# Shared key and value blocks loaded once, queries and stores issued at another place in the step, in a fused attention and mixture-of-experts kernel

## The chip, the cores and the metric

The kernel runs on one core of one Trainium2 chip. The metric is the device time of one execution in microseconds (us); before the change it is 421.25 us, the median of three runs (419.26 to 423.34).

## The reference

Eight batches of eight heads, 576 positions, head size 64. Heads 0 to 3 attend to the last 32 positions, heads 4 to 7 to every fourth of the last 128. The result, seen as 4608 rows of 512, goes through a layer that skips some rows and sends each of the others to one of eight experts.

```python
scores = scale * np.matmul(q, k.transpose(0, 1, 3, 2))
mask_plain = (rel >= 0) & (rel < window)                                        # window = 32
mask_dil = (rel >= 0) & (rel < window * dilation) & (rel % dilation == 0)       # dilation = 4
attn = softmax(np.where(masks, scores, -1e9));  x = attn @ v                    # rows of B*S, H*D
do_compute = x @ w_skip > 0
e_idx = argmax(x[do_compute] @ w_gate);  gate_w = softmax(...)[e_idx]
out = x;  out[do_compute] += gate_w * (relu(x @ w1[e_idx]) @ w2[e_idx])
```

## The kernel before

**Attention, 24 steps.** A pair of batches (`bp`, four of them) has two halves: half 0 is the four heads with the plain window, half 1 the four dilated ones, whose positions are reordered so that their keys too lie side by side. A half is cut in three parts (`PARTS`), and a part is one step `t`: t = 0, 1, 2 is half 0 of the first pair, 3, 4, 5 its half 1, and so on. A step handles three groups of 64 queries; each block of 32 queries needs two blocks of 32 keys and of 32 values, its own and one before it. Inputs come from DRAM arranged by step (`laid_out`).

**Loads.** `load("kv", t)` (L143) issues two DMAs on SP that fill a tile `kvs[t % 3]` with the keys of step t and the values of step t - 2 (`LAG`); `load("q", t)` one DMA for the queries, into one of three buffers. Neighbouring groups use the same key or value block; before the change a block that a step needs twice at a border is stored twice in DRAM, and the blocks at the border of two parts are loaded by both steps. `share` (L158) copies the values that matmuls on the other half of the partitions need into a tile `shared`: ACT copies partitions 0 to 63 and POOL 64 to 127.

**A step.** The order is written out in `STEP` (L474): T transposes the weights of step t (`turn`: PE, copied out of PSUM by ACT); R computes the scores of t + 2 (`product`, L188); E is the exponential of t + 1 on ACT; V and v split a piece of expert weights (ACT, DVE); C is `share(t + 1)`; S masks and reduces the scores of t + 2 on DVE (L199, L202) and subtracts the maximum on POOL (L204); A sums the values (L246); X transposes the outputs of t - 1 (L302) and copies them by ACT to `xT`; D divides on DVE (L256 to L260); each w gives one piece of the router's work on the pair before. PE's last matmul of `sums(t)` is followed by L302, so L302 marks the start of the next step on PE.

**SP's order.** At the start of step t SP issues `load("kv", t + 4)`, `load("q", t + 4)`, up to eight stores of finished rows (`EACH`; a half 0 is stored whole in two DMAs, a half 1 in sixteen), and in steps 12 to 19 one piece of the first expert's weights (L900). SP issues in order. The kv load waits for `sums(t - 1)`, for the copies out of its tile, and every DMA on SP uses one of eight completion semaphores in rotation, so that it waits for the DMA issued eight before it to have landed.

**After the attention.** `finish` does the router's work on the last pair, fills its waits with the first expert's matmuls, and `Experts.run` does the other experts. `Router.prepare` makes the router's constants on POOL in three pieces, one each at the end of steps 1, 2 and 3.

Of the kernel before, what the change touches and what calls it, by code (L numbers as in the profile page):

```python
# [20 lines left out]
P = 128  # L21
# [5 lines left out]
W = 32  # L27
# [10 lines left out]
KN = 4 * max(KEYS)  # L38
NEG = -8.0e9
LAG = 2  # L40
EACH = 8
# [7 lines left out]
def window(half, g, sub):  # L49

    lower, upper = ((0, 2), (1, 2), (1, 3))[g] if half else (g, NB + g + sub)
    return slice(4 * half * sub + lower, 4 * half * sub + upper + 1, upper - lower)


def swapped(half, g, sub):
    return g % NB == 1 if half else sub == 0
# [46 lines left out]
class Attention:  # L103
# [7 lines left out]
    def __init__(self, tc, consts, qkv, out, prepare):  # L111
# [11 lines left out]
        self.shared = [self.kp.tile([P, 2, DN], F32, name=f"shared{i}") for i in range(3)]  # L123
# [19 lines left out]
    def load(self, kind, t):  # L143
# [8 lines left out]
        a = VN if kind == "k" else 0  # L152
        n = VN + 4 * KEYS[t // PARTS % 2] if "k" in kind and t < last else VN
        if t < last + LAG:
            for hh in range(2):
                self.nc.sync.dma_start(out=self.kvs[t % 3][hh::2, hh, a:n], in_=self.qkv[t][hh::2, QN + a:QN + n])

    def share(self, t):  # L158
# [4 lines left out]
        loaded, shared = self.loaded(t), self.shared[t % 3]  # L163
        n, up = (D + 1, 0) if t // PARTS % 2 else (2 * (D + 1), D + 1)
        for copy, rows, a in (nc.scalar.copy, slice(0, 64), n), (nc.gpsimd.tensor_copy, slice(64, P), up):
            copy(out=shared[rows].rearrange("c h (x d) -> c h x d", d=n),  # L166
                 in_=loaded[rows].rearrange("c h (x d) -> c h x d", d=2 * n)[:, :, :, a:a + n])

    def scores(self, half, t, g0):
# [7 lines left out]
        k = self.keys(t).rearrange("c h (r b s i) -> c h r b s i", r=2, b=2, i=W)  # L177
        ps = []

        def product():  # L180
            ps.append(self.ps.both("s"))
            for g in range(NB):
                for r in range(2):
                    n, j = divmod(2 * g + r, 4)
                    for b in range(2):
                        for sub in range(2):
# [3 lines left out]
                                rhs=k[:, :, r, b, window(half, g, sub)], start=True, stop=True,  # L190
# [21 lines left out]
    def values(self, t):  # L212

        if t // PARTS % 2:
            shared, loaded = (v.rearrange("c h (r b y x d) -> c h r b y x d", r=2, b=2, y=2, d=D + 1)
                              for v in (self.shared[t % 3], self.loaded(t)))
            return (0, 2, 1), lambda r, b, g, y: shared[:, :, r, b, y, 0] if g == 1 else loaded[:, :, r, b, y, g // 2]
        shared, loaded = (v.rearrange("c h (r b x d) -> c h r b x d", r=2, b=2, d=D + 1)
                          for v in (self.shared[t % 3], self.loaded(t)))
        return (0, 1, 2), lambda r, b, g, y: loaded[:, :, r, b, 1 + g] if y else (  # L220
            shared[:, :, r, b, g - 1] if g else loaded[:, :, r, b, 0])
# [103 lines left out]
    def run(self, router, experts, early, finish):  # L325
# [56 lines left out]
        product(1)  # L382
        for _ in range(3):
            shift(1)
# [1057 lines left out]
```

## Time and profile before

| | |
|---|---|
| time, median of three | 421.25 us |
| time of the profiled execution | 420.55 us, of which the span of its instructions is 418.5 us |
| attention, steps 0 to 23 on PE | 11.5 to 159.4 us |
| TensorE busy over the span | 380.8 us (91%) |
| VectorE, ScalarE, GpSimd busy | 64%, 51%, 33% |
| DMA | 88.92 MB, mean 212 GB/s |

A row of a timeline reads: start, duration of the whole merged row in us, engine, line, operation, output and inputs, shape, count, and in brackets how long the engine had been idle and what released it. SPq is SP's queue of DMA issues.

### The profile page before, as it was taken

What the parts mean: (1) busy time and instruction counts of PE and PEld (TensorE: products, weight loads), DVE (VectorE), ACT (ScalarE), POOL (GpSimd) and SP (SyncE); (2) the same over time, 40 slices, a digit from 0 to 9 for tenths busy, and PEclk for the clock granted to TensorE, in tenths of its full rate; (3) what the DMA queues carried; (4) which work ended last, traced back from release to release, by engine and by line L of the source; (5) the groups of instructions that cost most, each with busy time, mean ns of one, the idle gap of its engine ahead of it and who ended that gap; (6) DMA issues with size and microseconds to landing.
All of it is one profiled execution on the core that took longest, in us unless ns stands there. A gap on an engine that the chain in (4) does not pass through costs nothing.

```text
span 418.5 us, 11103 instructions
## 1 busy us (share of the span) xinstructions
PE 380.8 (91%) x4257; PEld 325.8 (78%) x4257; DVE 268.7 (64%) x552; ACT 211.9 (51%) x435; POOL 137.2 (33%) x213
## 2 busy tenths in 40 slices
PE   5888698799699858989999999999999999999993
PEld 3777567678577746877998899899889879898982
DVE  5766438968996894888544835726726837768540
ACT  6576456676568664615427125424515516456420
POOL 7884513574346431032207212112113113141001
PEclk9999889999889999999999999999999999999998
DMA  7989778978998866373756354473663664766001
GB/s 235 402 316 366 250 209 290 336 226 233 341 367 295 275 183 212 117 221 122 264 169 210 130 198 140 163 248 102 201 225 116 203 212 154 275 207 219 25 2 44
DMA packets 40101, 88.92 MB, mean 212 GB/s; under 512 B 5315, under 2 KB 14547, under 8 KB 38504
## 3 DMA queue, kind: packets, MB, share of 16 engines
q1 hardware_dynamic: 36424, 77.02, 55.4%
q0 software_dynamic: 3616, 11.11, 7.9%
q8 instruction: 35, 0.57, 0.5%
q14 instruction: 26, 0.21, 0.2%
HBM read 73.88 MB, written 14.75 MB: 212 GB/s over the span
## 4 chain that ended last, share of the span: by engine, by line
PE 52%; DVE 0%; POOL 0%; POOLq 0%; issue 0%
PE o L1099 25%; PE s L1028 23%; PE tp L1009 2%; PE tp L1051 1%; PE tp L1063 0%; DVE yo L1104 0%; POOL out_dram L997 0%; POOLq L1369 0%; DVE txl L1013 0%; PE s L855 0%
## 5 line engine op out<-in xcount | busy, mean ns | idle before, releaser
L1099 PE MATMUL o<-w,h 128*128 128x512 f32 (+2 forms) x320 | 103.8, 398 | 1.0 <-DVE h L1032 1.0
L997 POOL DMA_INDIRECT out_dram<-yo,write x21 | 22.5, 1070 | 154.5 <-DVE yo L1104 154.5
L1028 PE MATMUL s<-xh,w 128*128 128x256 f32 (+3 forms) x240 | 69.6, 307 | 0.5 <-DVE at_rows L771 0.5
L1028 PE MATMUL s<-xl,w 128*128 128x256 f32 (+3 forms) x240 | 69.4, 306 | 0.0
L1099 PEld LDWEIGHTS o<-w,h 128*128 128x128 f32 (+2 forms) x320 | 57.9, 184 | 14.1 <-DVE h L1032 1.4
L1031 ACT ACTIVATE h<-s 128x256 fp32r<-128x256 f32 (+3 forms) x60 | 25.9, 432 | 79.0 <-PE s L1028 54.1
L204 POOL TENSOR_TENSOR sm<-sm,mx 128x768 f32<-128x768 f32 (+1 forms) x25 | 36.0, 1439 | 39.8 <-DVE z L256 27.6
L1028 PEld LDWEIGHTS s<-xh,w 128*128 128x128 f32 x240 | 45.5, 190 | 1.1 <-DVE at_rows L771 0.6
L1028 PEld LDWEIGHTS s<-xl,w 128*128 128x128 f32 x240 | 45.5, 190 | 0.4
L188 PE MATMUL s<-kv,q 128*32 128x128 f32 x1152 | 38.7, 281 | 5.2 <-DVE sm L199 1.8
L991 POOL DMA_INDIRECT xg<-out_dram,read x24 | 26.0, 1081 | 50.8 <-DVE read L834 24.0
L916 DVE TENSOR_TENSOR w0l<-w0l,w 128x512 fp32r<-128x512 f32 x48 | 34.0, 709 | 12.3 <-ACT w L907 11.2
L188 PEld LDWEIGHTS s<-kv,q 128*32 128x32 f32 x1152 | 31.7, 112 | 11.4 <-issue 7.7
L246 PE MATMUL o<-kv,pT 128*32 128x130 f32 x768 | 35.4, 286 | 3.5 <-ACT pT L234 2.1
L916 DVE TENSOR_TENSOR w2l<-w2l,w 128x512 fp32r<-128x512 f32 x40 | 27.6, 690 | 14.4 <-ACT w L907 13.4
L916 DVE TENSOR_TENSOR w1l<-w1l,w 128x512 fp32r<-128x512 f32 x40 | 27.8, 694 | 13.5 <-ACT w L907 12.3
L1032 DVE SCALAR_TENSOR_TENSOR h<-s,h 128x256 fp32r<-128x256 f32 (+3 forms) x60 | 28.6, 476 | 11.8 <-ACT h L1031 11.7
L166 POOL COPY shared<-kv 64x1040 f32<-64x1040 f32 x24 | 26.6, 1108 | 25.8 <-DMA kv<-in_qkv_dram 18.7
L1104 DVE SCALAR_TENSOR_TENSOR yo<-o,gate,xg 128x512 f32<-128x512 f32 (+2 forms) x21 | 15.7, 749 | 29.1 <-PE o L1099 29.0
L246 PEld LDWEIGHTS o<-kv,pT 128*32 128x32 f32 x768 | 29.2, 114 | 5.2 <-ACT pT L234 2.8
L233 PE MATMUL tp<-ident,sm 128*128 128x128 f32 x144 | 24.2, 291 | 9.1 <-ACT xT L305 5.8
L1012 ACT CAST xh<-tp 128x256 fp32r<-128x256 f32 (+3 forms) x32 | 13.2, 417 | 37.4 <-PE tp L1009 37.2
(204 smaller groups left out, 755.3 us busy)
## 6 DMA issues: line engine op xcount, KB each, us to landing
kv<-in_qkv_dram SPq DMA_DIRECT2D x24, 516.0 KB, 6.5
w0l<-in_moe_w_dram SPq DMA_DIRECT2D x48, 256.0 KB, 4.4
w1l<-in_moe_w_dram SPq DMA_DIRECT2D x40, 256.0 KB, 3.9
w2l<-in_moe_w_dram SPq DMA_DIRECT2D x40, 256.0 KB, 4.2
kv<-in_qkv_dram SPq DMA_DIRECT2D x20, 484.0 KB, 5.4
q<-in_qkv_dram SPq DMA_DIRECT2D x24, 384.0 KB, 6.8
out_dram<-xh SPq DMA_DIRECT2D x8, 576.0 KB, 7.6
out_dram<-xh SPq DMA_DIRECT2D x24, 80.0 KB, 4.8
```

The source lines that it names most:

```text
L166: copy(out=shared[rows].rearrange("c h (x d) -> c h x d", d=n), in_=loaded[rows].rearrange("c h (x d) -> c h x d", d=2 * n)[:, :, :, a:a + n])
L188: nc.tensor.matmul(ps[0][p:p + W, n, 2 * KW * j:2 * KW * (j + 1)], lhsT=q[:, r, b, g, sub], rhs=k[:, :, r, b, window(half, g, sub)], start ...
L204: nc.gpsimd.tensor_tensor(out=part, in0=part, in1=top.unsqueeze(2).broadcast_to([P, n, KW, 2]), op=ALU.subtract)
L233: nc.tensor.transpose(out=tp[:, P * j:P * j + P], in_=sm[:, NB * n + j], identity=self.ident)
L246: nc.tensor.matmul(ps[0][p:p + W, n, 2 * (D + 1) * j:2 * (D + 1) * (j + 1)], lhsT=pT[:, m, p:p + W], rhs=v(r, b, g, sub), start=True, stop ...
L916: (engine or self.nc.vector).tensor_tensor(out=lo, in0=raw, in1=hi.bitcast(F32), op=ALU.subtract)
L991: self.nc.gpsimd.indirect_dma_start(out=xg, out_offset=None, in_=self.out[0:rows], in_offset=bass.IndirectOffsetOnAxis(ap=row, axis=0),)
L997: self.nc.gpsimd.indirect_dma_start(out=view, out_offset=bass.IndirectOffsetOnAxis(ap=row, axis=0), in_=yo, in_offset=None, bounds_check=N ...
L1028: nc.tensor.matmul(ps[0], lhsT=w(part, k, P * f, P), rhs=x[:, k], start=(i == 0), stop=(i == len(terms) - 1))
L1031: nc.scalar.activation(out=hh, in_=ps[0], func=AF.Relu)
L1032: return lambda: nc.vector.scalar_tensor_tensor(out=hl, in0=ps[0], scalar=0.0, in1=hh.bitcast(F32), op0=ALU.max, op1=ALU.subtract)
L1099: nc.tensor.matmul(ps[0][0:n], lhsT=h[:, ts], rhs=w(part, f, 0, DM), start=(i == 0), stop=(i == len(terms) - 1))
```

## The change

Every key block that a step needs is in its DRAM row once at most. The border block (half 0) or blocks (half 1) of a part that the part before has already loaded are no longer loaded: `follow` copies them on POOL from the tile of step t - 1 to that of step t, right behind the scores of t - 1, for parts 1 and 2 of each half. A kv DMA has 768 columns of keys for 896 (half 0) or 1024 (half 1), and in half 0 780 columns of values for 1040. `share` of a half 0 now copies all three value pairs: ACT 1560 columns for 1040, POOL 1040 and, in parts 1 and 2, 520 more from the tile of the step before. `shared` has two tiles for three. In half 0 `sums` uses `shared` for one of the two blocks of every group, so from its first matmuls on. `load("q", t + 5)` is issued behind the scores of t + 2, then up to six stores for eight and the piece of weights; at the start of a step SP issues only the kv load, until the last three steps. A half 0 is stored after each part, two DMAs each. The router's constants are made at the end of steps 3, 4 and 5. Masks and the arrangement in DRAM follow the new order of blocks (not shown).

```diff
-EACH = 8
+VS = (4 * NB * (D + 1), VN)
+NEW = 2 * NB
+KL = 4 * W * NEW
+EACH = 6
...
-        self.shared = [self.kp.tile([P, 2, DN], F32, name=f"shared{i}") for i in range(3)]
+        self.shared = [self.kp.tile([P, 2, VS[0]], F32, name=f"shared{i}") for i in range(2)]
...
-        a = VN if kind == "k" else 0
-        n = VN + 4 * KEYS[t // PARTS % 2] if "k" in kind and t < last else VN
+        a = VN if kind == "k" else VN - VS[(t - LAG) // PARTS % 2]
+        n = VN + KL if t < last else VN
...
+    def follow(self, t):
+
+        half = t // PARTS % 2
+        if t < B * PARTS and t % PARTS:
+            new, old = (self.kvs[i % 3][:, :, VN:].rearrange("c h (s k) -> c h s k", k=4 * W) for i in (t, t - 1))
+            self.nc.gpsimd.tensor_copy(out=new[:, :, NEW:NEW + 1 + half], in_=old[:, :, 1:NB + 2:NB] if half else
+                                       old[:, :, NB:NB + 1])
+
...
+        shared, loaded, older = (v.rearrange("c h (n x d) -> c h n x d", x=NB, d=D + 1) for v in (
+            self.shared[t % 2], *(self.loaded(i)[:, :, VN - VS[0]:] for i in (t, t - 1))))
+        nc.scalar.copy(out=shared[0:64].rearrange("c h n x d -> c h (n x d)"),
+                       in_=loaded[0:64].rearrange("c h n x d -> c h (n x d)"))
+        if t % PARTS:
+            nc.gpsimd.tensor_copy(out=shared[64:P, :, :, 0], in_=older[64:P, :, :, NB - 1])
...
-        return (0, 1, 2), lambda r, b, g, y: loaded[:, :, r, b, 1 + g] if y else (
-            shared[:, :, r, b, g - 1] if g else loaded[:, :, r, b, 0])
+                          for v in (self.shared[t % 2], self.loaded(t)[:, :, VN - VS[0]:]))
...
+        nc.vector.memset(self.shared[0][64:P], 0.0)
...
+        self.follow(1)
...
+        self.follow(2)
+        self.load("q", 4)
...
-            for kind in "kv", "q":
-                self.load(kind, t + 4)
-            due = len(stores) - EACH * (PARTS - 1 - part) if t < steps - 1 else 0
-            for _ in range(min(len(stores), max(EACH, due))):
-                stores.pop(0)()
+            self.load("kv", t + 4)
+            if t >= steps - PARTS:
+                for _ in range(min(len(stores), EACH)):
...
-            if WSTART <= t < WSTART + CHUNKS:
-                experts.load_next((2 * t - 2 * WSTART - (CHUNKS - 1) * (t >= WSTART + CHUNKS // 2),))
...
                     product(t + 2)
+                    self.follow(t + 3)
+                    self.load("q", t + 5)
+                    if t < steps - PARTS:
+                        for _ in range(min(len(stores), EACH)):
+                            stores.pop(0)()
+                    if WSTART <= t < WSTART + CHUNKS:
+                        experts.load_next((2 * t - 2 * WSTART - (CHUNKS - 1) * (t >= WSTART + CHUNKS // 2),))
...
-            if t:
+            if t >= PARTS:
...
-            if i == len(quads) - 1:
+            if half == 0 or i == len(quads) - 1:
                 stores += self.store_rows(bp, half, xh, g0, NB)
```

On SP, in step 13 (the kv loads of step 17, `kv_85`, and of step 18, `kv_83`), with what each row waits for (DMAHW0 to 7 are the eight completion semaphores); before, from the query load on:

```order
L149 DMA q<-in_qkv_dram 128x768 [waits DMAHW2_49]
L292 DMA out_dram<-xh 16x5x256 [waits DMAHW3_49]
L292 DMA out_dram<-xh 16x4x256 [waits DMAHW4_49]
L292 DMA out_dram<-xh 16x4x256 [waits DMAHW5_49]
L292 DMA out_dram<-xh 16x5x256 [waits DMAHW6_49]
L292 DMA out_dram<-xh 16x5x256 [waits DMAHW7_49]
L292 DMA out_dram<-xh 16x4x256 [waits DMAHW0_49]
L292 DMA out_dram<-xh 16x4x256 [waits DMAHW1_49]
L292 DMA out_dram<-xh 16x5x256 [waits DMAHW2_49]
L900 DMA w0l_1656<-in_moe_w_dram 128x512 [waits DMAHW3_49]
L156 DMA kv_83<-in_qkv_dram 64x1936 [waits PE_49,DMAHW4_49,Activation_49,Pool_49]
```

Between the query load and the next kv load stand eight stores and a piece of weights. The same place after the change:

```order
L159 DMA kv_85<-in_qkv_dram 64x1808 [waits PE_49,DMAHW7_49,Activation_49,Pool_49]
L159 DMA kv_85<-in_qkv_dram 64x1808 [waits DMAHW0_49]
L152 DMA q<-in_qkv_dram 128x768 [waits DMAHW1_49,PE_49]
L310 DMA out_dram<-xh 16x4x256 [waits DMAHW2_49]
L310 DMA out_dram<-xh 16x5x256 [waits DMAHW3_49]
L310 DMA out_dram<-xh 16x5x256 [waits DMAHW4_49]
L310 DMA out_dram<-xh 16x4x256 [waits DMAHW5_49]
L310 DMA out_dram<-xh 16x4x256 [waits DMAHW6_49]
L310 DMA out_dram<-xh 16x5x256 [waits DMAHW7_49]
L926 DMA w0l_1735<-in_moe_w_dram 128x512 [waits DMAHW0_49]
L159 DMA kv_83<-in_qkv_dram 64x1808 [waits PE_49,DMAHW1_49,Activation_49,Pool_49]
```

Six stores stand there for eight, the query load also waits for PE (the scores whose buffer it takes), and the next kv load shares its semaphore, DMAHW1, with that query load.

On POOL, in steps 12 and 13 (copies for `share`, the router's `place` of the pair before, the subtraction L204); before:

```order
L166 COPY shared_87<-kv_83 64x1040
L808 TENSOR_TENSOR atf<-hot,first 128x72
L810 TENSOR_TENSOR rs<-rs,atf 128x9 x8
L812 TENSOR_SCALAR far<-sc 128x9
L814 TENSOR_TENSOR rs<-rs,far 128x9
L815 CAST place<-rs 128x9
L204 TENSOR_TENSOR sm<-sm,mx 128x768
L166 COPY shared_88<-kv_84 64x1040
L204 TENSOR_TENSOR sm<-sm,mx 128x768
```

and after (L185 and L186 are the two copies of `share`, L166 is now `follow`):

```order
L185 COPY shared_87<-kv_85 64x8x65
L186 COPY shared_87<-kv_83 64x8x130
L834 TENSOR_TENSOR atf<-hot,first 128x72
L836 TENSOR_TENSOR rs<-rs,atf 128x9 x8
L838 TENSOR_SCALAR far<-sc 128x9
L840 TENSOR_TENSOR rs<-rs,far 128x9
L841 CAST place<-rs 128x9
L223 TENSOR_TENSOR sm<-sm,mx 128x768
L166 COPY kv_84<-kv_83 128x2x256
L185 COPY shared_86<-kv_83 64x8x65
L186 COPY shared_86<-kv_84 64x8x130
L223 TENSOR_TENSOR sm<-sm,mx 128x768
```

The copies before a subtraction have grown from one to three.

## Rows read from the trace of the kernel before

**Rows 1.** Chain that ended last, by line, share of the span (page, part 4).
```profile
PE o L1099 25%; PE s L1028 23%; PE tp L1009 2%; PE tp L1051 1%; PE tp L1063 0%; DVE yo L1104 0%; POOL out_dram L997 0%; POOLq L1369 0%; DVE txl L1013 0%; PE s L855 0%
```

**Rows 2.** Stretches: length, busy per engine, granted clock, DMA share, GB/s.
```profile
11.50:42.20 30.70, 26.65 (x640) 22.36 (x636) 19.67 (x32) 20.94 (x36) 22.25 (x47) 1.00 0.97 364
42.20:84.20 42.00, 33.86 (x695) 26.98 (x693) 27.93 (x61) 23.87 (x50) 15.46 (x12) 0.92 0.82 269
84.20:122.70 38.50, 33.43 (x712) 27.85 (x710) 31.38 (x67) 24.92 (x53) 17.80 (x23) 0.91 0.89 283
...
195.50:418.50 223.00, 216.04 (x1229) 192.17 (x1228) 124.88 (x223) 92.97 (x195) 47.87 (x70) 0.99 0.50 165
```

**Rows 3.** Timeline of SP's queue, steps 12 to 14.
```profile
83.92 1.32 SPq L156 DMA_DIRECT2D kv<-in_qkv_dram  x2
...
85.98 6.45 SPq L292 DMA_DIRECT2D out_dram<-xh  x8
...
93.06 2.00 SPq L156 DMA_DIRECT2D kv<-in_qkv_dram  x2
...
103.21 1.12 SPq L156 DMA_DIRECT2D kv<-in_qkv_dram  x2
...
105.61 1.18 SPq L156 DMA_DIRECT2D kv<-in_qkv_dram  x2
```

**Rows 4.** Timeline of PE, steps 12 to 16.
```profile
86.11 1.52 PE L188 MATMUL s<-kv,q 128*32 128x128 f32 x48
...
88.89 0.87 PE L302 MATMUL tp<-ident,xh 128*128 128x128 f32 x6
...
95.80 0.88 PE L302 MATMUL tp<-ident,xh 128*128 128x128 f32 x6
...
102.16 0.87 PE L302 MATMUL tp<-ident,xh 128*128 128x128 f32 x6
...
111.94 0.90 PE L233 MATMUL tp<-ident,sm 128*128 128x128 f32 x3 [3.87 <-ACT xT L305]
112.77 2.79 PE L188 MATMUL s<-kv,q 128*32 128x128 f32 x48
...
119.96 1.52 PE L188 MATMUL s<-kv,q 128*32 128x128 f32 x48
```

**Rows 5.** Timeline of ACT, step 15.
```profile
110.44 1.07 ACT L166 COPY shared<-kv 64x1040 f32<-64x1040 f32 x1 [3.38 <-DMA kv<-in_qkv_dram]
```

**Rows 6.** Two stretches behind a wait of PE, columns as in rows 2.
```profile
50.50:57.00 6.50, 6.50 (x39) 3.57 (x43) 1.36 (x3) 3.19 (x8) 0.55 (x1) 0.55 0.75 235
...
111.90:118.00 6.10, 6.06 (x100) 5.07 (x100) 6.00 (x7) 3.55 (x6) 2.81 (x2) 0.52 1.04 354
```

**Rows 7.** DMA issues of the page: count, KB each, median us to landing.
```profile
kv<-in_qkv_dram SPq DMA_DIRECT2D x24, 516.0 KB, 6.5
...
kv<-in_qkv_dram SPq DMA_DIRECT2D x20, 484.0 KB, 5.4
```

**Rows 8.** Timeline of PE, step 22.
```profile
148.68 0.55 PE L233 MATMUL tp<-ident,sm 128*128 128x128 f32 x3 [1.18 <-ACT xT L305]
```

**Rows 9.** Timeline of PE, step 6.
```profile
50.50 0.42 PE L246 MATMUL o<-shared,pT 128*32 128x130 f32 x1 [3.46 <-issue]
```

**Rows 10.** Timeline of PE, step 0.
```profile
13.38 1.52 PE L188 MATMUL s<-kv,q 128*32 128x128 f32 x48 [0.74 <-DMA q<-in_qkv_dram]
```

**Rows 11.** Groups by form, 11 to 160 us: count, busy, mean ns, idle before.
```profile
L166 POOL COPY shared<-kv 64x1040 f32<-64x1040 f32 x24 | 26.6, 1108 | 25.8 <-DMA kv<-in_qkv_dram 18.7 <-PE tp L302 3.2 <-DMA out_dram<-xh 3.1
L166 ACT COPY shared<-kv 64x1040 f32<-64x1040 f32 x24 | 25.5, 1062 | 7.5 <-DMA kv<-in_qkv_dram 7.5
```

**Rows 12.** POOL's copy at 68.5 us and line L793: ns min/median/max, first start.
```profile
68.54 1.06 POOL L166 COPY shared<-kv 64x1040 f32<-64x1040 f32 x1
...
L793 DVE TENSOR_TENSOR vals<-gates x4: 178/178/848, 68.8 to 184.4; 128x9 bf16<-128x9 f32 x4
```

**Rows 13.** Line L149, the 24 query loads, from issue to landing.
```profile
DMA to landing us min/median/max: 4.5/6.8/8.6
```

More of the change, by code (lines that the diff above doesn't have):

```diff
@@ L49, in window @@
 def window(half, g, sub):
-    lower, upper = ((0, 2), (1, 2), (1, 3))[g] if half else (g, NB + g + sub)
-    return slice(4 * half * sub + lower, 4 * half * sub + upper + 1, upper - lower)
+    own, other = ((0, NEW - 2 * sub), (0, 2), (1, 2))[g] if half else (g, NEW - g - sub)
+    return slice(NB * half * sub + own, NB * half * sub + other + 1, other - own)
 def swapped(half, g, sub):
-    return g % NB == 1 if half else sub == 0
+    return g % NB != 1 if half else sub == 0
 def dilated_runs(g0, ng=NB):
@@ L162, in share @@
             return
[L163 to L167, printed above, removed]
+        if t // PARTS % 2:
+            loaded, shared = self.loaded(t), self.shared[t % 2][:, :, 0:DN]
+            for copy, rows, x in (nc.scalar.copy, slice(0, 64), 0), (nc.gpsimd.tensor_copy, slice(64, P), 1):
+                copy(out=shared[rows].rearrange("c h (n d) -> c h n d", d=D + 1),
+                     in_=loaded[rows].rearrange("c h (n x d) -> c h n x d", x=2, d=D + 1)[:, :, :, x])
+            return
+        shared, loaded, older = (v.rearrange("c h (n x d) -> c h n x d", x=NB, d=D + 1) for v in (
[4 more added lines that the diff above has]
+            nc.gpsimd.tensor_copy(out=shared[64:P, :, :, 0], in_=older[64:P, :, :, NB - 1])
+        nc.gpsimd.tensor_copy(out=shared[64:P, :, :, 1:], in_=loaded[64:P, :, :, 0:NB - 1])
     def scores(self, half, t, g0):
@@ L1278, in near @@
         return t.unsqueeze(1).unsqueeze(1)
[L1280 removed]
+    nearp, neard = near("nearp", lambda sub: swapped(0, 0, sub)), near("neard", lambda sub: True)
     nc.vector.tensor_copy(out=maskp, in_=nearp.broadcast_to(full))
@@ L1292, in make_masks @@
     g, bnd = divmod(RL, W)
-    assert swapped(1, g, 0) and not swapped(1, g + 1, 0) and not swapped(1, 0, 0)
+    assert not swapped(1, g, 0) and swapped(1, g + 1, 0) and swapped(1, 0, 0)
     for p in range(0, P, W):
-        nc.gpsimd.memset(maskd[p:p + W, 0, :, 0:W], NEG)
-        for a, n in ((0, bnd), (W, W)):
+        nc.gpsimd.memset(maskd[p:p + W, 0, :, W:KW], NEG)
+        for a, n in ((W, bnd), (0, W)):
             md = maskd[p:p + W, g, :, a:a + n]
@@ L1299, in make_masks @@
                                     channel_multiplier=-1, compare_op=ALU.is_ge, fill=NEG)
-        nc.gpsimd.memset(maskd[p:p + W, g + 1, :, 0:bnd], NEG)
+        nc.gpsimd.memset(maskd[p:p + W, g + 1, :, W:W + bnd], NEG)
     yield maskd
```

29 lines of the change are left out of this document (15 added, 14 removed).

## Prediction

> **What bounds the kernel now.** I read the chain that ended last first [rows 1]: nearly all that it names is PE on the expert lines L1099 and L1028, and none of it is attention. A table of stretches says why [rows 2]: from 195.5 us to the end PE is busy 216.0 of 223.0 us, and the change touches nothing there. The attention stands ahead of this chain, so what it saves or costs moves the rest as a block. I take one us of attention as one us of time.
>
> The attention's four stretches of six steps (the last of them ends at 159.4 us) are read in the same table. In the first (30.7 us) PE is busy 26.7 us and the DMA share is 0.97 at 364 GB/s: the transfers set the pace. The second is 42.0 us long with PE at 33.9, the third 38.5 us with PE at 33.4 and DVE at 31.4. So PE idles 4.1, 8.1 and 5.1 us in these three, and that idle time, with the lower clock behind some of it, is nearly all that a change of loads can win.
>
> Next, the waits inside. In the third stretch PE stands 3.87 us before L233 of step 16 [rows 4], released by ACT, and ACT had stood 3.38 us before its share copy for the kv load [rows 5]. SP's queue shows where the load was [rows 3, 4]: PE begins steps 13, 14 and 15 at 88.89, 95.80 and 102.16, but SP issues their kv loads at 93.06, 103.21 and 105.61, thus 4.2, 7.4 and 3.5 us late, because eight stores (6.45 us) stand ahead of each of the first two. Then PE's clock falls: granted 0.52 over 111.9 to 118.0 [rows 6], the lower of its two levels for nearly all of it, and L188 takes 2.79 us for 1.52 [rows 4].
>
> **The change part by part.**
>
> Late kv loads, third stretch. From kv issue to kv issue SP needs 93.06 - 83.92 = 9.1 us with eight stores [rows 3]. A store is 6.45 / 8 = 0.81 us, so with six it needs 7.5 us. In step 12 the query load now waits for the scores, which end at 86.11 + 1.52 = 87.6 [rows 4]; with 0.6 us for the query, 4.8 for six stores and 0.6 for the weights the next kv load is at 93.6, and the two after it at 101.1 and 108.6. Against the same PE times they are 4.7, 5.3 and 6.4 us late: the peak falls from 7.4 to 6.4 us, and stays longer, since a pair now has 22 stores for 18. The late load is smaller, 387 KB for 484 twice [rows 7] (64 partitions of 1548 columns for 1936), which is 0.2 MB or 0.5 us at 364 GB/s. So 1.5 us of the 3.87 go. I add the 1.3 us that L188 alone lost to the clock, because the rest of the wait comes in shorter pieces. Gain 2.8 us; at stake 0 to 5.1.
>
> Last stretch. The same pattern ends in a wait of 1.18 us at 148.68 [rows 8]. I take all of it, 1.2 us, since little but value-only loads is left then; 0 to 1.2.
>
> Second stretch. PE stands 3.46 us in the middle of `sums` of step 6, released by nothing that the profile shows ("issue") [rows 9], and the clock is at 0.55 over the next 6.5 us [rows 6]. All data were there, so it is PE's instructions that came late; step 6 is the first whose DMAs include eight stores. I price the clock as in the other case, 1.3 us, so 4.8 us are at stake. Six stores and smaller loads in front make it less likely, but nothing in the change removes it. I take half, 2.4 us; bounds -2 (such a stall elsewhere) and 4.8.
>
> First stretch. Six steps load 3 x 128 + 3 x 256 key columns and 3 x 260 value columns less, 1932 x 4 bytes x 128 partitions = 0.99 MB, at 364 GB/s [rows 2] 2.7 us; the wait of 0.74 us for a query in step 0 [rows 10] is a part of it. But POOL, busy 22.3 of 30.7 us, gets more (below), and `sums` of a half 0 now wants `shared` at once. The constants that move behind step 3 give POOL room where it is fullest. I take 1.6 us; bounds -2 and 2.7.
>
> ACT's longer copy. 1040 columns take 1.06 us [rows 11], so 1560 take 1.59: 0.53 us more in each of 12 steps, 6.4 us. In the third stretch ACT is busy 24.9 of 38.5 us [rows 2], so most of it falls in its idle time; the copy delays PE where PE waits for ACT to empty a PSUM tile. I take a fifth, 1.3 us; bounds 0 and 6.4.
>
> POOL's copies. POOL moves 1040 columns in 1.11 us [rows 11], which is about 1.07 ns a column. `follow` has 256 columns (0.27 us) eight times and 512 (0.55) eight times, the second copy of `share` 520 (0.55) eight times: 11.0 us, of which a quarter is in the first stretch and counted there. Elsewhere POOL is under half busy and the subtraction L204 has a whole step before it is needed. What remains is DVE. The router's L793 takes 178 ns in the median but once 848, and that one, begun at 68.79, ends with POOL's copy of 68.54 to 69.60 [rows 12]. That is 0.67 us for one of the 24 copies; if one in ten of the 24 new ones did the same it would cost 1.6 us, if none, 0. I take 0.9 us; bounds 0 and 3.
>
> The Trainium skill speaks against the change here (page "SBUF — State Buffer", section "SBUF: two separate sides"): the read and write port pair that VectorE and GpSimd share is an exclusive lock, and an operation with two SBUF inputs on VectorE is fully blocked while a GpSimd operation holds it. The trace's one slow L793 agrees. By the rule alone every new POOL microsecond that meets such an operation would be lost, at most the 8 us outside the first stretch, and the sum would be about 7 us worse; by the row it is 0.9.
>
> Moves that I cost at nothing: the query load behind the scores (it is still two steps ahead of its use, and the work of those two steps hides it), the extra memset of `shared` (DVE waits in the prologue for POOL's masks), the router's constants (first used in step 7). Uncovered, the first would cost what step 0 shows, 0.74 us a time.
>
> Sum: 2.8 + 1.2 + 2.4 + 1.6 = 8.0 gained, 1.3 + 0.9 = 2.2 lost, net 5.8. The profiled execution took 420.55 us (span 418.5, and 2.05 around it), 0.7 below the median of 421.25. So 420.55 - 5.8 = 414.8 us.
>
> **The rivals.**
>
> Hidden anyway. DVE is busy 31.4 of 38.5 us in the third stretch; if the router's work on DVE sets the pace, and instruction stalls come back at another place, only the first stretch and some of the late load remain, about 4.2 - 2.2 = 2 us: 418.5 us. For it speaks DVE's 82%; against it that PE is as full and waits for a load by name.
>
> Slower: the query's landing now gates the kv load. Every SP DMA waits for the one eight before it. With six stores and a piece of weights that is, for the next kv load, the query load of the same step, issued 1.4 us behind kv. If a query takes L to land, kv loads come no closer than 1.4 + L. At the 6.8 us of the median [rows 13] that is 8.2, and the loads are at 93.6, 101.8 and 110.0, the last 7.8 us late, about the old peak of 7.4. At the 8.6 us of the slowest it is 10.0: the last load is at 113.6, 11.4 us late and 4.0 more than the old peak; the same in the last stretch, half of it in the second, where no weights are loaded, makes 10 us. With the costs and the first stretch's gain, 420.55 + 10 + 2.2 - 1.6 = 431 us. It decides from L = 6.6 us, where the last load is 7.4 us late. Against it: fewer bytes stand ahead of a query.
>
> Full relief. If kv never comes late and the instruction stall goes, the gains are 5.1 + 1.2 + 4.8 + 2.7 = 13.8, less 2.2: 409 us.
>
> **How the numbers follow.** Forecast 0.45, hidden 0.28, slower 0.14, full relief 0.13. One per cent, 4.2 us, is about what a measurement of this kernel can tell from no change; below 417.0 is faster, above 425.5 slower. Nearly all of the forecast and all of full relief are faster, but its ACT and POOL terms can push a little of the forecast over the line: faster 0.56, same 0.30, slower 0.14. The range leaves out the slower rival and a little at the lower end: 407 to 422 us.
>
> **What would show it.** Right: SP's kv issues in steps 13 to 16 at most some 6 us behind PE, POOL's and ACT's waits for kv (18.7 and 7.5 us in all [rows 11]) at about half, attention ending near 153.7 us, and the first stretch below 30 us at a lower DMA share. Wrong: kv issues about ten us apart behind query landings; ACT's 1560-column copy as PE's releaser in most half-0 steps; long "issue" idles of PE again; or a wait at `sums` for `shared` in the first steps.

## The result, and the profile after

The change made no difference that can be told from the runs. The changed kernel takes 420.82 us (median of 20 runs, 417.60 to 424.65), the kernel before 420.69 (20 runs beside it, 412.84 to 430.88); the ratio of the comparison is 1.0102, 95% interval 1.0068 to 1.0136. That ratio, which has the change a per cent slower, counts only the runs near a kernel's fastest, and as those of the kernel before spread over 18 us, the one at 412.84 alone moves it by some 0.8%; I therefore go by medians and means over all runs, by which the difference is 0.1 us (means 421.07 and 420.95 with standard errors 0.44 and 0.88). By neither reading is there a gain. The forecast was 414.8.

The stretches of the changed kernel, cut as in [rows 2] (length, busy time of PE, PEld, DVE, ACT and POOL, granted clock, DMA share, GB/s):

```profile
11.50:42.20 30.70, 26.43 (x604) 22.26 (x608) 17.96 (x28) 21.23 (x36) 23.73 (x46) 0.94 0.93 312
42.20:84.20 42.00, 36.20 (x817) 29.50 (x813) 32.60 (x68) 29.50 (x63) 23.46 (x30) 1.00 0.88 274
84.20:122.70 38.50, 30.25 (x674) 24.37 (x666) 31.32 (x65) 25.85 (x52) 21.22 (x30) 1.00 0.89 277
195.50:418.50 223.00, 216.80 (x1232) 192.47 (x1230) 125.59 (x224) 93.52 (x197) 47.35 (x70) 1.00 0.50 165
```

In the first stretch the DMA share fell from 0.97 to 0.93, but PE did not get further. In the second PE is busier (36.2 us for 33.9) at the full clock. In the third it is less busy for the same 38.5 us, while DVE stays at 31.3.

SP's kv issues in steps 13 to 16, timeline of its queue (for [rows 3]):

```profile
89.09 2.19 SPq L159 DMA_DIRECT2D kv<-in_qkv_dram  x2
97.15 1.12 SPq L159 DMA_DIRECT2D kv<-in_qkv_dram  x2
105.60 1.16 SPq L159 DMA_DIRECT2D kv<-in_qkv_dram  x2
112.82 1.17 SPq L159 DMA_DIRECT2D kv<-in_qkv_dram  x2
```

PE begins steps 13 to 16 at 85.29, 92.19, 100.34 and 105.01 in this trace, so the loads are 3.8, 5.0, 5.3 and 7.8 us late. How much of that anyone waits for is in the groups by form, 11 to 160 us (for [rows 11]; count, busy time, mean ns, idle before and by whom it was ended):

```profile
L182 ACT COPY shared<-kv 64x1560 f32<-64x1560 f32 x12 | 17.9, 1491 | 2.0 <-DMA kv<-in_qkv_dram 2.0
L177 POOL COPY shared<-kv 64x1040 f32<-64x1040 f32 x12 | 13.3, 1110 | 3.1 <-DMA kv<-in_qkv_dram 1.3 <-PE o L264 1.3
L177 ACT COPY shared<-kv 64x1040 f32<-64x1040 f32 x12 | 12.9, 1072 | 1.8 <-DMA kv<-in_qkv_dram 1.8
L186 POOL COPY shared<-kv 64x1040 f32<-64x1040 f32 x12 | 12.8, 1069 | 3.8 <-PE w L794 1.7 <-DMA kv<-in_qkv_dram 1.7 <-issue 0.3
L185 POOL COPY shared<-kv 64x520 f32<-64x520 f32 x8 | 6.0, 747 | 0.5
L651 PE MATMUL tp<-ident,lt 128*128 128x128 f32 x27 | 4.6, 285 | 3.3 <-DVE sc L653 3.3
```

POOL's and ACT's waits for kv, 26.2 us before, are 6.8 in share's copies (1.3 + 1.7 + 2.0 + 1.8). They have gone as forecast, but the time has not fallen with them. The last row is the one that matters in the end: the router's transposes wait 3.3 us for `sc`, the tile into which VectorE reduces what they wrote. Before the change the same group was:

```profile
L625 PE MATMUL tp<-ident,lt 128*128 128x128 f32 x27 | 4.3, 283 | 1.9 <-DVE sc L627 1.9
```

Where PE stands, from its timeline:

```profile
13.88 1.52 PE L207 MATMUL s<-kv,q 128*32 128x128 f32 x48 [1.43 <-POOL kv L166]
24.68 2.72 PE L207 MATMUL s<-kv,q 128*32 128x128 f32 x48
...
94.71 0.55 PE L651 MATMUL tp<-ident,lt 128*128 128x128 f32 x3 [1.32 <-DVE sc L653]
95.62 0.55 PE L651 MATMUL tp<-ident,lt 128*128 128x128 f32 x3 [0.36 <-DVE sc L653]
96.62 0.85 PE L251 MATMUL tp<-ident,sm 128*128 128x128 f32 x6 [0.46 <-DVE sc L653]
...
150.65 1.96 PE L264 MATMUL o<-kv,pT 128*32 128x130 f32 x32 [2.82 <-issue]
...
166.47 0.77 PE L1035 MATMUL tp<-ident,xg 128*128 128x128 f32 x5 [0.50 <-DMA xg<-out_dram,read]
```

PE enters the second stretch 1.4 us later than before (43.59 for 42.23). The wait for `follow` behind the masks on POOL shows no part in that, since PE begins step 2 at 20.68 us, before at 20.77; step 2 itself takes 8.0 us for 5.5, with scores at the lower clock (2.72 us for 1.52). PE is 6.6 us ahead at the start of step 17 (111.37 for 117.99), and has lost nearly all of that when the attention ends (158.07 for 158.69). Of the loss, 5.4 us are in steps 17 and 18 (15.4 us for 10.0), in which DVE is busy 14.1 us, and 1.2 us in step 20, where there are three short waits for DVE's `sc` like the three shown of step 14. An instruction stall of 2.82 us in step 22, like the one of [rows 9] at another place, is made up for by a shorter step 23.

### The profile page after: what moved, and what is told of

Same layout as the page of the kernel before. It is cut to its first block, busy times and chain, and to the rows that moved or that the text cites. A ratio compares the mean times of both kernels' runs of the same rounds, so it can differ in the third digit from the quotient of the medians.

```text
span 419.0 us, 11169 instructions
## 1 busy us (share of the span) xinstructions
PE 380.0 (91%) x4257; PEld 324.7 (77%) x4257; DVE 271.8 (65%) x553; ACT 216.9 (52%) x435; POOL 149.4 (36%) x237
## 4 chain that ended last, share of the span: by engine, by line
PE 52%; DVE 0%; POOL 0%; POOLq 0%; issue 0%
PE o L1125 25%; PE s L1054 23%; PE tp L1035 2%; PE tp L1077 1%; PE tp L1089 0%; DVE yo L1130 0%; POOL out_dram L1023 0%; POOLq L1395 0%; DVE txl L1039 0%; PE s L881 0%
## 5 line engine op out<-in xcount | busy, mean ns | idle before, releaser
L1125 PEld LDWEIGHTS o<-w,h 128*128 128x128 f32 (+2 forms) x320 | 57.9, 184 | 14.1 <-DVE h L1058 1.4
L1017 POOL DMA_INDIRECT xg<-out_dram,read x24 | 25.1, 1048 | 50.5 <-DVE read L860 17.3
L942 DVE TENSOR_TENSOR w0l<-w0l,w 128x512 fp32r<-128x512 f32 x48 | 33.4, 697 | 12.3 <-ACT w L933 11.3
L264 PE MATMUL o<-kv,pT 128*32 128x130 f32 x672 | 34.2, 284 | 7.6 <-issue 2.8
L942 DVE TENSOR_TENSOR w1l<-w1l,w 128x512 fp32r<-128x512 f32 x40 | 27.7, 693 | 13.9 <-ACT w L933 12.7
L264 PEld LDWEIGHTS o<-kv,pT 128*32 128x32 f32 x672 | 28.3, 113 | 9.4 <-issue 8.1
L251 PE MATMUL tp<-ident,sm 128*128 128x128 f32 x144 | 23.8, 286 | 8.4 <-ACT xT L339 2.9
L227 ACT ACTIVATE sm<-sm 128x768 f32<-128x768 f32 (+1 forms) x25 | 20.6, 823 | 18.4 <-POOL sm L223 18.2
```

The costliest lines, as they stand in the source:

```text
L227: nc.scalar.activation(out=sm[:, a:a + n], in_=sm[:, a:a + n], func=AF.Exp, scale=0.125)
L251: nc.tensor.transpose(out=tp[:, P * j:P * j + P], in_=sm[:, NB * n + j], identity=self.ident)
L264: nc.tensor.matmul(ps[0][p:p + W, n, 2 * (D + 1) * j:2 * (D + 1) * (j + 1)], lhsT=pT[:, m, p:p + W], rhs=v(r, b, g, sub), start=True, stop ...
L942: (engine or self.nc.vector).tensor_tensor(out=lo, in0=raw, in1=hi.bitcast(F32), op=ALU.subtract)
L1017: self.nc.gpsimd.indirect_dma_start(out=xg, out_offset=None, in_=self.out[0:rows], in_offset=bass.IndirectOffsetOnAxis(ap=row, axis=0),)
L1125: nc.tensor.matmul(ps[0][0:n], lhsT=h[:, ts], rhs=w(part, f, 0, DM), start=(i == 0), stop=(i == len(terms) - 1))
```

## Experiments

Beside each group of runs the kernel before was timed on the same chip, and the groups ran on several chips. Medians and means cover all runs, means with their standard errors (a run of 941.74 us and one of 2052.5 us are left out of the means).

| run | runs | median | mean | before beside it, median | ratio of the comparison |
|---|---|---|---|---|---|
| loads | 6 | 421.13 | 421.0 ± 1.5 | 421.86 | none given |
| order | 6 | 420.41 | 420.4 ± 0.5 | 421.86 | none given |
| bytes | 6 | 415.98 | 416.6 ± 0.8 | 421.86 | none given |
| bytesorder | 6 | 413.93 | 413.7 ± 1.0 | 421.60 | 0.9899 (0.9788 to 1.0010) |
| keysonly | 12 | 418.21 | 418.1 ± 0.9 | 420.69 | 0.9969 (0.9888 to 1.0050) |
| valsonly | 12 | 422.84 | 422.2 ± 1.0 | 420.69 | 0.9986 (0.9901 to 1.0072) |
| followlate | 12 | 423.58 | 423.6 ± 0.5 | 420.69 | 1.0220 (1.0147 to 1.0293) |
| keysact | 12 | 416.74 | 416.4 ± 0.5 | 421.60 | 0.9967 (0.9919 to 1.0014) |
| keyspool | 12 | 421.66 | 421.0 ± 0.7 | 421.60 | 1.0102 (1.0038 to 1.0166) |
| keysdve | 12 | 417.93 | 418.2 ± 0.6 | 421.60 | 1.0063 (1.0005 to 1.0121) |
| beforerot | 7 | 420.12 | 418.8 ± 1.4 | 419.90 | 1.0117 (1.0023 to 1.0211) |
| afterrot | 12 | 415.82 | 416.4 ± 0.8 | 419.90 | 0.9965 (0.9916 to 1.0014) |
| keyspoolrot | 12 | 417.02 | 417.0 ± 0.5 | 419.90 | 1.0018 (0.9966 to 1.0071) |
| keysonlyrot | 12 | 417.00 | 417.2 ± 0.6 | 419.90 | 1.0030 (0.9987 to 1.0073) |
| aftersame | 11 | 420.62 | 420.6 ± 0.7 | 420.70 | 1.0029 (0.9978 to 1.0079) |
| afterrotdve | 12 | 417.90 | 418.2 ± 0.6 | 420.70 | 0.9998 (0.9956 to 1.0041) |

### The parts of the change

**loads**: the changed kernel with the old order on SP.

```diff
-EACH = 6
+EACH = 8
...
-            self.load("kv", t + 4)
+            for kind in "kv", "q":
+                self.load(kind, t + 4)
...
```

> The loads, follow and share of the changed kernel with the old order on SP: kv and query load at the start of a step, then up to eight stores and the weights there, a half 0 stored whole, router's constants from step 1 on. The theory 'given back by the copies' (the smaller and earlier loads win some 5 us, and the new POOL and ACT copies in front of the subtraction and the exponential take as much): about the time before, ratio 0.995 to 1.005, with the exponential's wait for POOL's subtraction between 11 and 160 us near the 15.4 us of the changed kernel. The rival 'the order costs' (stores by thirds, queries behind the scores and late constants lose what the loads win): ratio 0.988 or less. The rival 'hidden anyway' (VectorE and PE's own instruction stalls set the pace): ratio 0.996 to 1.004, with the waits for kv gone and the same idle time of PE under other names, mostly VectorE and issue.

**order**: the kernel before with the new order on SP.

```diff
-EACH = 8
+EACH = 6
...
+                    self.load("q", t + 5)
...
```

> The kernel before with the new order on SP alone: query load behind the scores, then up to six stores and the weights, a half 0 stored by thirds, constants from step 3 on. 'Given back by the copies': the order alone takes away part of the late kv load and nothing pays for it, ratio 0.990 to 0.997, kv waits of POOL and ACT together (26.2 us before) at 15 to 20. 'The order costs': ratio 1.008 or more, and the finish behind the attention longer by about 1.5 us, as in the changed kernel. 'Hidden anyway': 0.997 to 1.003.

**bytes** and **bytesorder**: narrower loads with nothing copied in place of what is missing, in the old and in the new order.

```diff
-        a = VN if kind == "k" else 0
-        n = VN + 4 * KEYS[t // PARTS % 2] if "k" in kind and t < last else VN
+        a = VN if kind == "k" else VN - VS[(t - LAG) // PARTS % 2]
+        n = VN + KL if t < last else VN
```

> The kernel before, whose kv loads are cut to the widths of the changed kernel, with nothing copied in place of what is missing, so that the keys and values of the border blocks are old data (the output is not the attention's). It keeps the old order on SP. It has the gain of fewer bytes and none of the costs of the copies. 'Given back by the copies': ratio 0.983 to 0.992. 'Hidden anyway': 0.996 to 1.003, although kv waits fall below 15 us. 'The order costs': as the run with the loads and copies in the old order, 0.985 to 0.990.

> The kernel before with both the new order on SP and the loads cut to the new widths, and no copies in place of what is missing (border blocks are old data, the output is not the attention's). It is the whole gain of the change without its copies, with the router's work as before. 'Given back by the copies', and the order worth something: 412.5 to 415 us, attention ended near 151 us. If the order is worth nothing: 415.5 to 417, as the cut loads alone (415.98). If the order loses: above 417.

The loads with their copies gain nothing (421.13 beside 421.86), the order alone 1.4 us by the medians, less than its spread can tell, and fewer bytes alone 5.9. Together, without copies, they gain 7.7 us (421.60 to 413.93; 6.9 by the means). "Hidden anyway" fell with these two. The forecast had 8.0 for this sum. One expectation failed with them: the exponential's wait for POOL's subtraction (5.0 us before, 15.4 in the changed kernel) is 13.9 us in bytesorder, which has no copies and is the fastest, so that wait is not what the copies cost.

**nocopy** and **nocopy2**: the changed kernel without the copies that it adds, in all steps and from step 2 on.

```diff
-        if t < B * PARTS and t % PARTS:
+        if False and t < B * PARTS and t % PARTS:
...
```

> The changed kernel without its added copies: follow does nothing, POOL's second copy of share is left out and ACT's copy has 1040 of its 1560 columns, so border blocks are old data (the output is not the attention's); order on SP as changed. 'Given back by the copies': ratio to the kernel before 0.983 to 0.992, the exponential's wait for POOL falls from 15.4 us to about the 5 us of before, and VectorE's and PE's waits with it. 'Hidden anyway': within 0.995 to 1.003, with the exponential's wait gone and PE idle for VectorE or issue instead. 'The order costs': 1.000 to 1.008.

> The changed kernel without its added copies from step 2 on (follow never, POOL's second copy of share and ACT's 520 more columns only in steps 0 and 1, so that shared holds finite values and no expert overflows; border blocks are old data). It repeats the run without copies, whose router sent more rows to one expert than its capacity and added a stage to the end, so that only its attention (ended 7.2 us before that of the changed kernel) could be read. 'Given back by the copies': 413 to 415.5 us, ratio 0.980 to 0.987, attention ended near 151 us. Rival, 'a lucky execution' (executions of one kernel differ by some 10 us, and the attention's end in one profile is one draw): ratio 0.99 to 1.0.

With old data in the border blocks the router sends more rows to an expert than it has room for, and a stage for the rows left over follows (654.1 and 612.62 us), so the times say nothing. Their attention ended at 150.84 and 153.89 us for 158.07, 7.2 and 4.2 us earlier. This is one profile of each, but it points where bytesorder does: with the copies the gain is gone. The exponential's wait, which was to fall to about 5 us, is 13.7 us in nocopy.

### Which copy

**keysonly** keeps the new keys and `follow`, with the values of before; **valsonly** the new values and their copies, with the keys of before.

```diff
-VS = (4 * NB * (D + 1), VN)
+VS = (VN, VN)
```

(keysonly, with `share` and `values` of before for a half 0.)

> The changed kernel with its key loads and follow, but the values of a half 0 loaded, shared and summed as before (1040 columns, ACT's and POOL's one copy of 1040). It keeps 1152 of the 1932 columns that six steps save, and of the added copies the 16 of follow alone. 'Given back by the copies', most of it by share's (POOL's second copy and ACT's longer one stand in front of the subtraction and the xT copies in the half-0 steps): 416 to 418.5 us, ratio 0.986 to 0.993. If follow is the costly one: 420 to 422. If any POOL time costs alike (a copy stretches VectorE's operations): in between, 418 to 420.

> The kernel before with the new order on SP and the values of a half 0 as changed (780 columns loaded, ACT's copy of 1560 and POOL's two); keys as before, no follow. It saves 780 of the 1932 columns and has all of share's added copies. 'Given back by the copies', most of it by share's: 420 to 422.5 us, ratio 0.997 to 1.004. If follow is the costly one: 416 to 418.5. If any POOL time costs alike: 418.5 to 421.

The loss is on the side of the values: 418.21 and 422.84 us, the second a little above its range.

**followlate** moves `follow` behind the subtraction.

```diff
-                    self.follow(t + 3)
...
+                elif op == "F":
+                    self.follow(t + 3)
```

> The changed kernel with follow of a step behind the subtraction of that step on POOL, at the step's end, instead of ahead of the share copies and the subtraction. The copies are the same, only their place moves. If POOL's place in front of the subtraction is what costs: 418 to 419.5 us, 1 to 2.5 below the changed kernel's 420.8, and the exponential's wait for the subtraction (15.4 us) falls below 12. If a copy costs because it stretches VectorE's operations or fills POOL wherever it stands: 420 to 421.5, no gain.

Neither expectation held. The exponential's wait for POOL fell from 15.4 to 8.9 us, so that wait had not been the path, and the kernel is slower. Its group of the scores, 11 to 160 us:

```profile
L207 PE MATMUL s<-kv,q 128*32 128x128 f32 x1056 | 36.1, 288 | 15.2 <-POOL kv L166 15.2
```

PE now waits 15.2 us for the moved copy, against 1.4 in the changed kernel. The old place was the better one.

**keysact** and **keyspool** add to keysonly one idle copy each: on ACT as much time as the longer copy costs, on POOL the second copy of `share`.

```diff
+        nc.scalar.copy(out=self.spare[0:64], in_=loaded[0:64, :, 0:138])
```

```diff
+        if t % PARTS:
+            nc.gpsimd.tensor_copy(out=self.spare[64:P], in_=older[64:P, :, 2:15:4])
```

> The kernel with new keys and old values (418.2 us), plus one idle copy on ACT of 64x276 right behind share's copy in every half-0 step: as much ACT time (about 0.43 us, twelve times, 5.2 us in all) as the changed kernel's copy of 1560 columns has over that of 1040. Nothing else uses what it writes. If ACT's longer copy is what the value part loses: 420 to 422 us. If POOL's second copy is: 417.5 to 419. If it takes both, at the places where the two come together: 418.5 to 419.5.

> The kernel with new keys and old values (418.2 us), plus one idle copy on POOL of 64x520 ahead of share's in the half-0 steps of parts 1 and 2, read from the value tile of the step before, as the changed kernel's second copy of share (8 times 0.75 us). If POOL's second copy is what the value part loses: 420 to 422 us. If ACT's longer copy is: 417.5 to 419. If it takes both: 418.5 to 419.5.

ACT's 5.2 us cost nothing that shows (416.74 beside 418.21, below all three expectations). POOL's eight copies cost 3.5 us by the medians (421.66; 2.9 ± 1.1 by the means), of the 4.6 between keysonly and valsonly. Taken alone this convicts the copy.

**keysdve**: keysonly with `follow` of steps 1 and 2 on VectorE.

```diff
-            self.nc.gpsimd.tensor_copy(out=new ...
+            (self.nc.vector if t < NB else self.nc.gpsimd).tensor_copy(out=new ...
```

> The kernel with new keys and old values (418.2 us), whose follow of steps 1 and 2 runs on VectorE, since in its profile PE waits 1.62 us at 13.88 for POOL's follow behind the masks. If POOL's queue at the start is a term of its own: that wait below 0.8 us and 416.5 to 417.7 us, the first step's end near 20 us for 20.8. If the first steps wait for transfers anyway: 418 to 419, with the wait under another name (a query or key load).

The wait for `follow` is gone, the time is not lower (417.93); in this profile PE waits 1.8 us for a query's landing instead.

### The PSUM tile

The router's transposes waited for `sc` about as long as the kernels were slow. The group, 11 to 160 us, of keysonly:

```profile
L649 PE MATMUL tp<-ident,lt 128*128 128x128 f32 x36 | 5.5, 282 | 2.8 <-DVE sc L651 2.8
```

and of keyspool, which differs by the idle copies alone:

```profile
L653 PE MATMUL tp<-ident,lt 128*128 128x128 f32 x27 | 4.5, 283 | 4.4 <-DVE sc L655 4.4
```

The copy touches neither the router nor PSUM, so I compared what the instructions wait for; DVE_49, Activation_49 and Pool_49 are the semaphores of VectorE, ACT and POOL. For one turning of the router (nine transposes, three into each of three tiles of `tp`, each tile read by DVE, then the next `turn`) PE has, with the first transpose into each tile, before:

```text
L625 MATMUL tp<-ident,lt 128x128 [waits Activation_49]
L625 MATMUL tp<-ident,lt 128x128 [waits Activation_49]
L625 MATMUL tp<-ident,lt 128x128 [waits DVE_49]
L233 MATMUL tp<-ident,sm 128x128 [waits Activation_49,Pool_49]
```

and after:

```text
L651 MATMUL tp<-ident,lt 128x128 [waits Activation_49]
L651 MATMUL tp<-ident,lt 128x128 [waits DVE_49]
L651 MATMUL tp<-ident,lt 128x128 [waits DVE_49]
L251 MATMUL tp<-ident,sm 128x128 [waits DVE_49,Activation_49]
```

The code asks for one of three `tp` tiles each time. Which one it gets is fixed when the program is built, and in the changed kernel a transpose gets the tile that the one ahead of it has just filled. Over the three turnings in the attention, the transposes that wait for DVE, of these nine, number two before, in order, bytes, bytesorder and both runs without copies; three in keysonly, keysact and keysdve; four in the changed kernel, loads and valsonly; five in keyspool. (The twelve of an expectation below count a fourth turning, behind the attention.) Of the kernels with narrower loads, those with two or three stand at 414 to 418 us, those with four or five at 421 to 423; followlate has none and is slow for its own reason.

The test takes the tiles in fixed rotation, after which none waits for DVE there.

```diff
-            name, bufs = ("tp", 3) if name == "tp" else ("w", 1)
+            name, bufs = (f"tp{next(self.turns) % 3}" if name == "tp" else "w"), 1
```

**beforerot**, **afterrot**, **keyspoolrot** and **keysonlyrot** are four kernels with this edit.

> The kernel before whose three PSUM tiles for transposes (tp) are taken in fixed rotation, instead of the one that the recording layer's own model of time has free first. In the kernel before, two of the twelve router transposes L625 wait for VectorE to have read the one just ahead; in rotation none does. Theory 'PSUM tile chosen at build time': PE's waits for sc go from 1.9 us to near 0 and the time falls by about 2 us, ratio 0.992 to 0.998. If those waits are covered by VectorE anyway (it is late behind them): ratio 0.998 to 1.002.

> The changed kernel with the three tp tiles in fixed rotation. In it four router transposes wait for VectorE to have read the one just ahead (PE's waits for sc 4.2 us), in rotation none. Theory 'PSUM tile chosen at build time': about 4 us below the changed kernel's 420.8, thus 416 to 417.5, and more below it than the kernel before in rotation is below its own (2 us). Theory 'POOL's copies themselves': 419 to 421, with the waits for sc gone and PE waiting as long under another name.

> The kernel with new keys, old values and the idle second copy on POOL (421.66 us), tp in fixed rotation. Its waits for sc are 6.6 us (five transposes behind VectorE), against 2.8 in the kernel without that copy (418.2 us): the difference of 3.8 is all that the copy cost. Theory 'PSUM tile chosen at build time': within 1 us of the next kernel (the same without the copy, in rotation), both 415 to 417. Theory 'POOL's copy itself': 3 us or more above the next kernel.

> The kernel with new keys and old values (418.2 us), tp in fixed rotation: three transposes behind VectorE go to none, waits for sc from 2.8 us to near 0. Theory 'PSUM tile chosen at build time': 415 to 416.5 us. If the waits are covered anyway: 417.5 to 418.7. It is also the candidate for a version below both kernels.

The changed kernel falls to 415.82 us, by the means 4.7 ± 0.9 below itself (timed in two groups). Its group of the router's transposes:

```profile
L651 PE MATMUL tp<-ident,lt 128*128 128x128 f32 x27 | 4.2, 285 | 0.0
```

POOL's idle copy costs nothing that shows any more: 417.02 with it and 417.00 without. Both lie just above the theory's ranges. (The 6.6 us of waits that the expectation of keyspoolrot quotes are 5.3 in keyspool's profile, 4.4 before the transposes and 0.9 before `turn`, so the copy brought 2.5 us of waits and not 3.8.) For the kernel before the expected 2 us did not come; the medians show no gain, and its seven runs are too few to tell 1 or 2 us. PE's timeline of afterrot at the place where the changed kernel had three waits:

```profile
92.87 0.88 PE L320 MATMUL tp<-ident,xh 128*128 128x128 f32 x6
93.59 1.39 PE L651 MATMUL tp<-ident,lt 128*128 128x128 f32 x9
95.43 0.84 PE L251 MATMUL tp<-ident,sm 128*128 128x128 f32 x6 [0.45 <-POOL sm L223]
```

The nine transposes go in one piece. From L320 to `turn` it is 2.56 us; in the changed kernel 92.19 to 96.62, 4.43. Summed over the three turnings this stretch is 7.9 us before, 9.7 in keysonly, 11.3 in the changed kernel and 12.2 in keyspool; in rotation it is 7.6 to 8.0 in all four kernels. So the rotation takes 3.7 us off the changed kernel there and 0.3 off the kernel before, where `turn` then waits for POOL's subtraction instead. The profiled execution of afterrot took 420.79 us, so its gain as a whole is in its other runs and not in this profile: step 18 alone takes 10.45 us there (6.9 in bytesorder), at a granted clock of 0.67.

**aftersame** keeps the rotation and puts such waits back, six where the changed kernel has four: all transposes of a turning share a tile.

```diff
-            g_ps = self.ps.tile([P, 512], F32, name="tp", bufs=3)
+            g_ps = self.ps.tile([P, 512], F32, name="tp" if j0 == 0 else "same", bufs=3)
```

> The changed kernel with tp in fixed rotation (415.8 us), except that the router's second and third transposes of a turning (L651) go through the same PSUM tile as its first, so that each waits for VectorE's read of the one ahead: six such waits in the attention, where the changed kernel has four and the rotation none. Theory 'PSUM tile chosen at build time': the loss comes back, 419.5 to 422 us, waits for sc at 5 to 7 us. If it was something else in the rotation that helped (another tile's wait): 415 to 417 us, although the waits for sc come back.

The loss comes back: 420.62 us, with a stretch from L320 to `turn` of 11.3 us in the three turnings again, and in its group:

```profile
L652 PE MATMUL tp<-ident,lt 128*128 128x128 f32 x27 | 4.8, 285 | 4.9 <-DVE sc L654 4.9
```

**afterrotdve** is afterrot with `follow` of steps 1 and 2 on VectorE, by the same line as keysdve.

> The changed kernel with tp in fixed rotation (415.8 us) and follow of steps 1 and 2 on VectorE instead of POOL, whose queue there is full of masks (PE waits 1.83 us for follow in the profile of the rotation, 1.43 in the changed kernel). If this wait and the lower clock that follows it in the changed kernel's first steps are a term of their own: 413.5 to 415 us, the wait gone. If transfers set the first steps anyway: 415 to 417.

417.90 us, above both expectations: the wait at the start is gone and is no term of its own. Why the time is 2.1 us above afterrot (1.8 ± 1.0 by the means) is not shown; it may be spread. Beside this run, timed in the same group, aftersame is 2.7 us slower (2.4 ± 0.9 by the means), less than beside afterrot. The fastest complete version is afterrot, 415.82 us beside 419.90 (3.6 ± 1.0 by the means), with all of the change in it; its ratio of the comparison (0.9965) does not tell it from the kernel before.

## Why the prediction was wrong

**What bounds the kernel; late loads.** Right in the main. The waits for kv fell to a quarter, kv issues stayed within 5.3 us of PE up to step 15 and reached 7.8 in step 16, where I had 6.4 as the worst. The rival by which a query's landing paces them did not come. The kv issues are 7.2 to 8.5 us apart, which that rival allows too, but between 80 and 124 us SP waits only 0.5 us for a query's landing ahead of them; its own issues fill the time. The other signs failed: the first stretch did not get shorter, and the attention ends at 158.07 us, not near 153.7.

**The gains as a sum** (2.8 + 1.2 + 2.4 + 1.6 = 8.0 us). Right in sum: 7.7 in bytesorder by the medians, 6.9 ± 1.2 by the means. How it divides among the four is not shown; the first stretch lost 1.4 us in the changed kernel's profile, where I had a gain of 1.6, and instruction stalls moved (2.82 us at 150.65 for 3.46 at 50.50) where I took half of one as gone. In steps 17 and 18, where the changed kernel loses 5.4 us, bytesorder too takes 13.9 us for the 10.0 of before, with DVE busy 13.2 of them; I read this as VectorE's work taking back there, without any copies, part of what earlier loads gave.

**ACT's longer copy** (1.3 us). Nothing measurable, by keysact. The copy takes 1.49 us, not 1.59.

**POOL's copies** (0.9 us). This is the step that failed. I asked whom a longer POOL queue delays, found the subtraction covered and only DVE's port at stake. In detail this was off, since the added copies took 14.9 us (4.0 + 4.9 + 6.0) and not 11.0, and [rows 12] is one of twelve stretched operations of the kernel before (last section), not the only one. For what the copies cost PE at run time it was about right: keyspoolrot and keysonlyrot differ by nothing, so the 7 us that the prediction gives by the rule alone did not come either. But adding them changed the program elsewhere: transposes of the router got the PSUM tile that VectorE had still to read, and PE waits there. aftersame against afterrot puts 4.8 us on these waits by the medians (4.2 ± 1.0 by the means), and the rotation takes 5.0 off the changed kernel. In the profiles, the stretches from L320 to `turn` grew by 3.4 us from the kernel before to the changed one. I had no term for waits of instructions that the diff does not touch. With the rotation the time is 1.0 us from the forecast; that is near in part by luck, since the next paragraph's loss is in that time and had no price. The orders of instructions that I quoted show waits, but I read them for SP and POOL only.

**Moves costed at nothing.** One was not free: the order on SP. From the end of the attention to the end of the span it is 259.6 to 259.9 us in the four profiles with the old order, and 260.9 to 263.5 in those with the new one (nocopy and nocopy2 left out): 1.1 us more in the changed kernel (260.9 for 259.8), 3.0 more in afterrot (262.8). So an us of attention was not quite an us of time. A part of it is a wait. In all four profiles with the old order PE does not wait for the gathered rows `xg` behind the attention; in every one with the new order it does, 0.5 us in the changed kernel and up to 2.46 in afterrotdve. PE's timeline of order, and then of keysonly:

```profile
165.32 0.77 PE L1013 MATMUL tp<-ident,xg 128*128 128x128 f32 x5 [0.93 <-DMA xg<-out_dram,read]
```

```profile
160.50 0.76 PE L1033 MATMUL tp<-ident,xg 128*128 128x128 f32 x5 [1.74 <-DMA xg<-out_dram,read]
```

In the changed kernel SP issues its last ten stores from 164.29 us on, in the kernel before its last eight from 166.86. That these delay the gather was not tried.

**The rivals.** "Hidden anyway" named a time near the result (418.5), by luck: bytes and bytesorder refute its mechanism for the kernel as a whole, since with the loads alone the time falls. Only in steps 17 and 18 may VectorE set the pace. That a wait on VectorE took the place of the loads is true, but of the router's transposes, through a tile chosen at build time, not through VectorE's 82%. The slower rival and full relief did not come.

**What stays open.** The waits for `sc` in the changed kernel's profile are 3.3 us before L651 and some 0.9 before L251; the rest of the 5.0 may be what follows from them, or spread. Of the 6.0 us between the forecast and the result, the profiles put 3.4 on the router's stretches and 1.1 behind the attention; the remainder is not assigned. Why the building of the program chooses another tile when a POOL copy is added is not shown, only that it does.

## What to carry to other kernels

A change can cost time at instructions that it does not touch: compare the waits of the whole engine that bounds the kernel, before and after, above all where tiles come from a pool that chooses. An idle copy that costs time does not yet convict the copy; repeat it with the tiles fixed. Price what follows a reordered queue too: here the part behind the attention grew in every profile with the new order.

## What the runs showed of the hardware

VectorE operations with two inputs were stretched where they met a POOL operation, and more often than [rows 12] let expect. In the changed kernel DVE's L674 takes 0.99 us, four times the 0.23 of its shortest: it begins while POOL's copy of 96.87 runs and ends at 98.06, 0.09 us behind it. In bytesorder the same operation (L654) meets none. The Trainium skill (page "SBUF — State Buffer", section "SBUF: two separate sides") calls the port pair that the two engines share an exclusive lock, on which a VectorE operation with two SBUF inputs fully blocks while a GpSimd operation that reads SBUF holds it; this row agrees. The changed kernel's timelines of DVE and POOL:

```profile
97.07 0.99 DVE L674 SCALAR_TENSOR_TENSOR key<-d,revf 128x72 f32<-128x72 f32 x1
...
96.87 1.10 POOL L177 COPY shared<-kv 64x1040 f32<-64x1040 f32 x1
```

and bytesorder's of DVE:

```profile
91.95 0.23 DVE L654 SCALAR_TENSOR_TENSOR key<-d,revf 128x72 f32<-128x72 f32 x1
```

Counting in the attention (11.5 to 160 us) every DVE operation over 100 ns longer than the shortest of its form, there are 12 with 6.9 us in all before and 16 with 8.4 us after, each beside a POOL operation and each with two inputs. In the changed kernel 6.6 us of this stand beside the old copy L177, 0.5 beside added copies alone. In keyspoolrot there are 13 with 7.7 us and in keysonlyrot 12 with 5.4, at 417.02 and 417.00 us: as far as these two show, PE does not wait for it.
